# Block-causal attention and two expert layers on one core: head B's key blocks in reversed order

## The chip, the core and the metric

The kernel runs on one core of a Trainium2 chip. The metric is the time of one execution on the device in microseconds, median of three runs. The engines, named as in the profile, are PE (matmuls; PEld is its weight load), DVE and ACT (vector and scalar engine; both read and write PSUM, the matmuls' output memory of eight banks), POOL (elementwise work in SBUF) and SP (it only issues DMAs here).

## What is computed

Four batches of eight heads, 576 positions, 64 values a head. A query block of 64 sees the key blocks up to its own. The result goes through two expert layers.

```
scores = scale * q @ k.T          # per batch and head, 576 x 576
scores = where(block_i >= block_j, scores, -1e9)      # blocks of 64
attn = softmax(scores); x = (attn @ v), heads side by side: 2304 x 512
h = x @ w_in;  solu = h * softmax(h);  x = layernorm(solu) * g_ln @ w_out      # d_ff 1024
h = x @ w2_in; out = (h * tanh(softplus(h))) @ w2_out                          # d_ff 2048
```

## The kernel before, in words

**A planner sets the order.** The program adds operations with an engine, a cost, what they read and write, and a priority; `Plan.order` runs them through a list of events and emits every engine's instructions in the order that comes out. Priorities come from the table `PRIO` (lines 27 to 41) as base + step x index. On the chip each engine keeps its written order and waits by semaphores.

**Attention** (`pair`, line 533) works on two heads x = 0, 1 (A and B) of a batch at a time, 16 pairs. Loads (lines 539 to 558) bring q, k and v as 128 rows x 5 tiles x 2 heads x 64. `turn` (566) transposes k and q on PE, both heads at once; ACT and DVE split them into a high and a low part. The queries are shifted by 64, so that query tile t (0 to 4) sees EXT[t] = 64, 192, 320, 448 or 576 keys, and its first 64 rows don't see the last 64 of these. Scores (`mm`, 586) take three matmuls each, head A on the upper 64 rows of the array and head B on the lower. DVE masks and takes the maximum (617 to 641), ACT takes the exponential (603), DVE sums and inverts (597, 599), POOL normalises (649).

**Packs.** The normalised probabilities of tile t and head x lie in a tile of EXT[t] + 64 columns, the last 64 zero (memset once, 513). PE transposes them in pieces of 128 x 128 (688), in the four packs of line 521, for each head apart: 4 + 4 + 4 + 3 pieces. ACT (698) or DVE (695) copies each pack from PSUM to `ptw`. The products with v (`pv`, 658 to 677) come in two groups, queries 0 to 319 behind the second pack and 320 to 575 behind the fourth; each product has 128 keys, and the two heads lie on 64 columns of the array each. All of this is in f32; the scores and the layers use fp32r.

**The layers.** Tiles of 128 positions go through the first layer (`moe1_tile`, lines 744 to 798; `moe1_x2`, 806) as soon as a batch's attention is done. Its weights, and those of the second layer, are 64-bit floats that ACT, DVE and POOL take apart and put together (`weight`, 377 to 452; 304, 310). The second layer (901, 919) runs in two halves; its first half's weights lie where attention's buffers were, so they open when the last pair is done.

## Time and profile before

| | us |
|---|---|
| median of three runs (lowest, highest) | 836.85 (836.77, 838.5) |
| profiled execution | 836.64 |
| its span, first to last instruction | 834.9 |
| PE busy | 806.3 |
| ACT, DVE, POOL busy | 437.3, 435.8, 272.8 |

The span is 1.7 us shorter than the execution's own time. PE's busy time counts the stretch in which at least one matmul is in flight; matmuls overlap, so the mean length of one is longer than the step to the next. The mean granted clock of PE is 0.996.

### The profile page before, as it was taken

To read this page: it belongs to the slowest core of one execution; us is meant where nothing else is said; L and a number is where in the kernel's file an instruction comes from. 1 tells how busy PE (TensorE), PEld (TensorE's weight loads), DVE (VectorE), ACT (ScalarE), POOL (GpSimd) and SP (SyncE) were. 2 spreads that over 40 slices of the span, in tenths; PEclk is the share of its full clock that TensorE was granted. 3 is DMA by queue.
4 is the path that set the end of the run, shared out by engine and by line. 5 is a ranking of instruction groups with operands and counts; after the bars stand their busy time and mean duration, and the time that the engine had idled before them with its cause. 6 is when DMAs were issued, how large, how long until landed. Compare 5 with 4: busy or idle time off the path is not lost.

```text
span 834.9 us, 13619 instructions
## 1 busy us (share of the span) xinstructions
PE 806.3 (97%) x5184; PEld 708.3 (85%) x5184; DVE 435.8 (52%) x845; ACT 437.3 (52%) x944; POOL 272.8 (33%) x338
## 2 busy tenths in 40 slices
PE   4789999999999999999999999999999999999998
PEld 4667778887887898989898898999999989999996
DVE  7899999766755335899815687311111122112121
ACT  5889698656654334666636776532424323323230
POOL 4669888642533322331113432310202202102000
PEclk9899999999999999999999999999999999999999
DMA  8744334222200103433114635202202023031121
GB/s 202 166 112 120 109 95 110 47 60 71 50 26 15 40 14 112 154 126 114 64 57 133 214 102 177 75 1 76 74 3 75 21 94 114 2 114 41 35 76 38
DMA packets 88369, 69.54 MB, mean 83 GB/s; under 512 B 64496, under 2 KB 75248, under 8 KB 88304
## 3 DMA queue, kind: packets, MB, share of 16 engines
q1 hardware_dynamic: 88304, 68.67, 28.1%
q8 instruction: 41, 0.67, 0.3%
q14 instruction: 24, 0.20, 0.1%
HBM read 54.50 MB, written 14.16 MB: 82 GB/s over the span
## 4 chain that ended last, share of the span: by engine, by line
PE 76%; DVE 11%; ACT 6%; DMA 3%; issue 2%; POOL 1%; SPq 0%; ACTq 0%; DVEq 0%; POOLq 0%
PE ps L901 23%; PE ps L919 22%; PE ps L744 8%; PE ps L806 8%; PE ps L665 4%; PE ps L688 4%; PE ps L591 4%; ACT pt L603 2%; PE ps L567 1%; PE ps L790 1%; DMA wraw<-in_moe_w_in_dram 1%; DVE st L758 1%; DVE ptw L695 1%; DVE ps L433 1%; DVE e L765 1%
## 5 line engine op out<-in xcount | busy, mean ns | idle before, releaser
L310 DVE TENSOR_TENSOR gl<-s,gh 128x384 fp32r<-128x384 f32 x96 | 61.7, 646 | 254.9 <-ACT gh L304 254.8
L910 ACT ACTIVATE s<-ps 128x384 f32<-128x384 f32 x96 | 46.8, 490 | 199.1 <-PE ps L901 198.8
L313 POOL TENSOR_TENSOR x2l<-x2r,x2h 128x384 fp32r<-128x384 f32 x48 | 51.1, 1100 | 234.7 <-ACT x2h L304 227.6
L649 POOL TENSOR_SCALAR pt<-pt,sm 128x320 f32<-128x320 f32 (+4 forms) x160 | 89.8, 584 | 62.3 <-DVE sm L599 55.3
L603 ACT ACTIVATE pt<-ps,nmx 128x576 f32<-128x576 f32 (+4 forms) x160 | 82.9, 542 | 13.7 <-DVE nmx L618 6.0
L806 PE MATMUL ps<-lth,woh 128*128 128x256 f32 x288 | 81.6, 283 | 1.2 <-DVE ltl L310 1.2
L806 PE MATMUL ps<-lth,wol 128*128 128x256 f32 x288 | 80.0, 278 | 0.0
L806 PE MATMUL ps<-ltl,woh 128*128 128x256 f32 x288 | 79.9, 278 | 0.0
L901 PE MATMUL ps<-x2h,w2iha 128*128 128x384 f32 x192 | 64.7, 337 | 1.1 <-ACT s L910 0.8
L901 PE MATMUL ps<-x2h,w2ila 128*128 128x384 f32 x192 | 64.5, 336 | 0.0
L901 PE MATMUL ps<-x2h,w2ilb 128*128 128x384 f32 x192 | 64.4, 335 | 0.0
L901 PE MATMUL ps<-x2h,w2ihb 128*128 128x384 f32 x192 | 64.4, 335 | 0.0
L901 PE MATMUL ps<-x2l,w2iha 128*128 128x384 f32 x192 | 64.3, 335 | 0.0
L901 PE MATMUL ps<-x2l,w2ihb 128*128 128x384 f32 x192 | 64.3, 335 | 0.0
L688 PE MATMUL ps<-ident,pt 128*128 128x128 f32 x480 | 60.5, 277 | 1.1 <-ACT pt L603 0.8
L688 PEld LDWEIGHTS ps<-ident,pt 128*128 128x128 f32 x480 | 53.3, 142 | 6.3 <-issue 3.3
L806 PEld LDWEIGHTS ps<-lth,woh 128*128 128x128 f32 x288 | 54.1, 188 | 3.7 <-DVE ltl L310 2.1
L665 PE MATMUL ps<-ptw,vraw 128*64 128x256 f32 (+2 forms) x512 | 56.8, 365 | 0.3 <-DVE ptw L695 0.2
L919 PE MATMUL ps<-w2oha,gl 128*128 128x512 f32 x144 | 56.5, 393 | 0.0
L919 PE MATMUL ps<-w2ola,gh 128*128 128x512 f32 x144 | 56.5, 392 | 0.0
L919 PE MATMUL ps<-w2ohb,gl 128*128 128x512 f32 x144 | 56.4, 392 | 0.0
L919 PE MATMUL ps<-w2olb,gh 128*128 128x512 f32 x144 | 56.4, 392 | 0.0
(114 smaller groups left out, 1983.2 us busy)
## 6 DMA issues: line engine op xcount, KB each, us to landing
wraw<-in_moe_w_in_dram SPq DMA_DIRECT2D x24, 512.0 KB, 4.3
wraw<-in_moe_w_out_dram SPq DMA_DIRECT2D x24, 512.0 KB, 3.8
x2r<-x_d SPq DMA_DIRECT2D x12, 768.0 KB, 4.7
kraw<-in_k_dram SPq DMA_DIRECT2D x31, 160.0 KB, 3.1
qraw<-in_q_dram SPq DMA_DIRECT2D x31, 160.0 KB, 3.2
x_d<-xo SPq DMA_DIRECT2D x18, 256.0 KB, 2.2
acc_d<-ob SPq DMA_DIRECT2D x18, 256.0 KB, 2.2
ac<-acc_d SPq DMA_DIRECT2D x18, 256.0 KB, 3.9
```

Source lines behind the costliest of these rows:

```text
L310: nc.vector.tensor_tensor(out=dst, in0=src, in1=hi.bitcast(F32), op=ALU.subtract)
L313: nc.gpsimd.tensor_tensor(out=dst, in0=src, in1=hi.bitcast(F32), op=ALU.subtract)
L591: nc.tensor.matmul(out=dst, lhsT=a.t[hs, t * P:(t + 1) * P], rhs=m.t[hs, c0:c1], start=(i == 0), stop=(i == 2))
L603: add(ACT, c_act(EXT[t], acc=True), lambda: nc.scalar.activation(out=pp.t[:, 0:EXT[t]] if t < 4 else pp.t[:, 0:EXT[t]].rearrange("p (a c) ...
L649: nc.gpsimd.tensor_scalar(pp, pp, sm.t[:, x, t:t + 1], 1.0, op0=ALU.mult, op1=ALU.mult)
L665: nc.tensor.matmul(out=ps(s)[x * D:(x + 1) * D, o:o + n_], lhsT=vr.t[:, j, x, :], rhs=packs[pi].t[:, x, a:a + n_], start=(i == 0), stop=(i ...
L688: nc.tensor.transpose(ps2(s)[:, x, i * P:(i + 1) * P], pts[t][x].t[:, j * P:(j + 1) * P], ident)
L744: nc.tensor.matmul(out=ps2(hp)[:, hf, :], lhsT=x.t[:, kk, :], rhs=w[:, kk, hf * 512:(hf + 1) * 512], start=bool(first), stop=bool(last))
L806: nc.tensor.matmul(out=ps(s)[:, (c % 2) * 256:(c % 2) * 256 + 256], lhsT=w[:, kk, cs], rhs=x.t[:, kk, :], start=(kk == 0 and i == 0), stop ...
L901: nc.tensor.matmul(out=h(), lhsT=w[wk][:, kk, ms], rhs=x.t[:, kk, :], start=(kk == 0 and i == 0), stop=(kk == KD - 1 and i == 2))
L910: add(ACT, c_act(G2), lambda: nc.scalar.activation(out=s.t, in_=h(), func=AF.Mish), r=[hk, LEFT], w=[s.key()], rel=[hp], prio=pri("f_v" + ...
L919: nc.tensor.matmul(out=ps(oslots[t]), lhsT=x.t[:, tsl], rhs=w[wk][:, m, :], start=(m == 0 and i == 0), stop=(m == n - 1 and i == 2))
```

## The change

Head B's keys are loaded with their blocks of 64 in reversed order (`load_k`), its values with the halves of each 128 rows swapped to match. For query tile t head B then uses the last EXT[t] key columns, and the block that is masked for half the rows lies first. Both heads' probabilities of a tile share one buffer of 2 x EXT[t] columns, A's ahead of B's, so that A's last block and B's last block lie side by side, and one 128 x 128 transpose turns both. The zero columns go, with their memsets. There are three packs of 8, 8 and 9 transposes; two are copied by ACT, one by DVE. One operation holds all products: six per head over 128 keys (`OFFS`), then for each tile and head one over 64 keys, head A on the first 64 rows and columns of the array and head B on the last 64 of both. It waits for all three packs and takes two banks. Scores of tiles 2 and 1 change places in their bank pair, and POOL normalises in the order 4, 3, 2, 1, 0. The table of priorities is another one throughout.

```diff
 PRIO = {
-    "load_k": (3504.94, 0.69), "load_q": (3601.34, 2.86), "load_v": (10764.44, 18.27), "tr": (1871.2, 0),
...
+    "load_k": (2508.37, 65.35), "load_q": (2386.26, 352.01), "load_v": (3551.6, 0.07), "tr": (2558.2, 60.53),
+    "te": (2672.56, 73.32), "sc": (3442.57, 0.01), "mx": (363.67, 453.95), "ex": (3739.18, 0.11),
...
@@ -501,16 +501,12 @@
         nc.vector.memset(kraw.tiles[i][64:128, QT - 1], 0.0)
-        nc.vector.memset(vraw.tiles[i][64:128, QT - 1], 0.0)
...
-    NPT, NPTW = (4, 4, 4, 4, 3), 5
-    pt_r = [Rot(at, f"pt{t}_", NPT[t], (P, EXT[t] + 64), F32) for t in range(QT)]
-    for t in range(QT):
-        for i in range(NPT[t]):
-            nc.vector.memset(pt_r[t].tiles[i][:, EXT[t]:EXT[t] + 64], 0.0)
+    NPT, NPTW = (2, 2, 2, 2, 2), 5
+    pt_r = [Rot(at, f"pt{t}_", NPT[t], (P, 2 * EXT[t]), F32) for t in range(QT)]
@@ -518,17 +514,24 @@
-    PACKS = [
-        [(0, 0), (1, 0), (2, 0), (2, 2)],
-        [(1, 1), (2, 1), (3, 0), (4, 0)],
-        [(3, 1), (4, 1), (3, 2), (4, 2)],
-        [(3, 3), (4, 3), (4, 4)],
-    ]
-    RUNS = (
-        (320, 0, [(0, 0, 64, 320, 0), (1, 1, 0, 256, 64), (2, 0, 384, 128, 192)]),
-        (256, 320, [(0, 1, 256, 256, 0), (1, 2, 0, 256, 0), (2, 2, 256, 256, 0), (3, 3, 0, 256, 0),
-                    (4, 3, 256, 128, 128)]),
+    PACKS = (
+        [(t, 0, x, x, (t - 1) * P) for x in range(2) for t in range(1, QT)],
+        [(t, 1, x, x, (t - 2) * P) for x in range(2) for t in range(2, QT)] + [(4, 3, x, x, 384) for x in range(2)],
+        [(t, 2, x, 0, (t - 3) * P + 256 * x) for x in range(2) for t in range(3, QT)]
+        + [(t, t, 2, 1, 64 * t) for t in range(QT - 1, -1, -1)],
     )
+    PACKW = (1024, 1024, 512 + 384)
+
+    OFFS = (
+        (0, 0, 0, ((0, 0), (1, 0)), 256, 64), (0, 1, 1, ((0, 0), (1, 0)), 128, 192),
+        (1, 0, 0, ((0, 256), (1, 256)), 256, 0), (1, 1, 1, ((0, 128), (1, 128)), 256, 0),
+        (1, 2, 2, ((0, 0), (0, 256)), 256, 0), (1, 3, 1, ((0, 384), (1, 384)), 128, 128),
+    )
+    RUNS = ((0, 320), (320, 256))
@@ -552,10 +555,31 @@
-        for tag, r, src, off, pad in (("load_k", kr, k, 0, False), ("load_q", qr, q, -64, False), ("load_v", vr, v, 0, True)):
+        def load_k():
+            blocks = k[b, 2 * h2 + 1].rearrange("(j p) d -> p j d", p=64)
+            nc.sync.dma_start(out=kr.t[0:64, :, 1, :], in_=blocks[:, 8::-2, :])
+            nc.sync.dma_start(out=kr.t[64:128, 0:4, 1, :], in_=blocks[:, 7::-2, :])
+
+        m, go = load(lambda: kr.t[:, :, 0, :], k, n0 * S, False)
+        add(SP, 0.92, go, w=[kr.key(0)], prio=pri("load_k", p))
+        add(SP, 1.06, load_k, w=[kr.key(1)], prio=pri("load_k", p))
+        for x in range(2):
+            rows = v[b, 2 * h2 + x]
+
+            def go(x=x, rows=rows):
+                if x:
+                    blocks = rows.rearrange("(j p) d -> p j d", p=64)
+                    nc.sync.dma_start(out=vr.t[64:128, :, 1, :], in_=blocks[:, 0:9:2, :])
+                    nc.sync.dma_start(out=vr.t[0:64, 0:4, 1, :], in_=blocks[:, 1:9:2, :])
+                else:
+                    nc.sync.dma_start(out=vr.t[:, 0:4, 0, :], in_=rows[0:512, :].rearrange("(j p) d -> p j d", p=P))
+                    nc.sync.dma_start(out=vr.t[0:64, 4, 0, :], in_=rows[512:S, :])
+
+            add(SP, 1.06, go, w=[vr.key(x)], prio=pri("load_v", p))
-        pts = [[x.next(), x.next()] for x in pt_r]
+        pts = [x.next() for x in pt_r]
...
+                    o = (S - EXT[t]) * x
+                    nc.tensor.matmul(out=dst, lhsT=a.t[hs, t * P:(t + 1) * P], rhs=m.t[hs, o + c0:o + c1],
...
-            pp = pts[t][x]
+            pp = pts[t]
             add(ACT, c_act(EXT[t], acc=True), lambda: nc.scalar.activation(
-                out=pp.t[:, 0:EXT[t]] if t < 4 else pp.t[:, 0:EXT[t]].rearrange("p (a c) -> p a c", a=2), in_=src(),
+                out=pp.t[:, x * EXT[t]:(x + 1) * EXT[t]] if t < 4
+                else pp.t[:, x * EXT[t]:(x + 1) * EXT[t]].rearrange("p (a c) -> p a c", a=2), in_=src(),
...
-        for ts in (((3, 0), (0, 448)), ((2, 0), (1, 320))):
+        for ts in (((3, 0), (0, 448)), ((1, 0), (2, 192))):
@@ -632,10 +658,15 @@
-            add(DVE, 0.105 * len(ms), lambda s=s, ms=ms: [nc.vector.memset(
-                ps2(s)[0:64, :, o + EXT[t] - 64:o + EXT[t]], NEG) for t, o in ms], w=[sk], prio=pri("mx", p))
+            def mask(t, o, s):
+                a, d = o + EXT[t] - 64, S - EXT[t]
+                nc.vector.memset(flat(s, a + 2 * d)[0:64, a:].rearrange("p (x c) -> p x c", x=2)[:, :, 0:64], NEG)
+
+            add(DVE, 0.105 * len(ms), lambda s=s, ms=ms: [mask(t, o, s) for t, o in ms], w=[sk], prio=pri("mx", p))
-        for t in (4, 3, 0, 2, 1):
+        for t in (4, 3, 2, 1, 0):
-
-        def pv(ri, w, c0, items):
-            s = Slot()
-            ok, xk = ("o", p, ri), xt.key(h2, ri)
-
-            def go():
-                for i, (j, pi, a, n_, o) in enumerate(items):
-                    for x in range(2):
-                        nc.tensor.matmul(
-                            out=ps(s)[x * D:(x + 1) * D, o:o + n_], lhsT=vr.t[:, j, x, :],
-                            rhs=packs[pi].t[:, x, a:a + n_], start=(i == 0), stop=(i == len(items) - 1))
-
...
-        for pi, pk in enumerate(PACKS):
-            w = len(pk) * P
+        for pi, (pk, w) in enumerate(zip(PACKS, PACKW)):
             th = ptw_r.next()
             s = Slot(2)
             sk = ("pT", p, pi)
 
-            def tr(s=s, pk=pk):
-                for i, (t, j) in enumerate(pk):
-                    for x in range(2):
-                        nc.tensor.transpose(ps2(s)[:, x, i * P:(i + 1) * P], pts[t][x].t[:, j * P:(j + 1) * P], ident)
-
-            add(PE, 0.218 * len(pk) + 0.1 * (len(pk) < 4), tr, r=[pts[t][x].key() for t, _ in pk for x in range(2)], w=[sk, th.key()],
+            def turns(s=s, pk=pk):
+                for t, j, x, a, o in pk:
+                    c = t if x == 2 else 2 * t - j if x else j
+                    nc.tensor.transpose(ps2(s)[:, a, o:o + P], pts[t].t[:, c * P:(c + 1) * P], ident)
+
...
-            a = 64 if pi == 0 else 0
-            if pi % 2:
-                add(DVE, c_dve(2 * (w - a)), lambda s=s, a=a, w=w, th=th: nc.vector.tensor_copy(
-                    th.t[:, :, a:w], ps2(s)[:, :, a:w]), r=[sk], w=[th.key()], rel=[s], prio=pri("pe", p))
+            if pi == 1:
+                add(DVE, c_dve(w), lambda s=s, w=w, th=th: nc.vector.tensor_copy(
+                    th.t.rearrange("p a c -> p (a c)")[:, 0:w], flat(s, w)), r=[sk], w=[th.key()], rel=[s], prio=pri("pe", p))
             else:
-                add(ACT, c_act(2 * (w - a)), lambda s=s, a=a, w=w, th=th: nc.scalar.activation(
-                    out=th.t[:, :, a:w], in_=ps2(s)[:, :, a:w], func=AF.Copy), r=[sk], w=[th.key()], rel=[s], prio=pri("pe", p))
+                add(ACT, c_act(w), lambda s=s, w=w, th=th: nc.scalar.activation(
+                    out=th.t.rearrange("p a c -> p (a c)")[:, 0:w], in_=flat(s, w), func=AF.Copy), r=[sk], w=[th.key()],
+                    rel=[s], prio=pri("pe", p))
...
-            for ri in range(2):
-                if pi == max(it[1] for it in RUNS[ri][2]):
-                    pv(ri, *RUNS[ri])
+
+        os_ = [Slot(), Slot()]
+        oks = [("o", p, 0), ("o", p, 1)]
+        xks = [xt.key(h2, 0), xt.key(h2, 1)]
+
+        def pv():
+            for i, (r, j, pi, at_, n_, o) in enumerate(OFFS):
+                for x, (a, c0) in enumerate(at_):
+                    nc.tensor.matmul(
+                        out=ps(os_[r])[x * D:(x + 1) * D, o:o + n_], lhsT=vr.t[:, j, x, :],
+                        rhs=packs[pi].t[:, a, c0:c0 + n_], start=(i in (0, 2)), stop=False)
+            for t in range(QT):
+                c0, r = (P * t, 0) if t < 3 else (P * t - 320, 1)
+                for x in range(2):
+                    hs = slice(x * D, (x + 1) * D)
+                    nc.tensor.matmul(
+                        out=ps(os_[r])[hs, c0:c0 + 64], lhsT=vr.t[hs, t, x, :],
+                        rhs=packs[2].t[hs, 1, 64 + 64 * t:128 + 64 * t], start=False, stop=(t in (2, 4)))
+
+        add(PE, 4 * 1600 / 2370.0 + 0.25, pv, r=[vr.key(0), vr.key(1)] + [x.key() for x in packs], w=oks + xks, acq=os_,
+            prio=pri("pv", p))
...
```

What the order of the instructions shows, at three places. On SP, the first DMAs of the program before (kraw, qraw, vraw hold a pair's k, q, v; wraw a piece of weights):

```order
L399 DMA wraw_88<-in_moe_w_in_dram 128x512
L399 DMA wraw_89<-in_moe_w_in_dram 128x512
L542 DMA kraw_94<-in_k_dram 128x5x64 x2
L542 DMA kraw_95<-in_k_dram 128x5x64 x2
L547 DMA qraw_92<-in_q_dram 64x64
L551 DMA qraw_92<-in_q_dram 128x4x64
L542 DMA qraw_92<-in_q_dram 128x5x64
L399 DMA wraw_88<-in_moe_w_in_dram 128x512
```

and after the change:

```order
L550 DMA qraw_92<-in_q_dram 64x64
L554 DMA qraw_92<-in_q_dram 128x4x64
L545 DMA qraw_92<-in_q_dram 128x5x64
L545 DMA kraw_94<-in_k_dram 128x5x64
L560 DMA kraw_94<-in_k_dram 64x5x64
L561 DMA kraw_94<-in_k_dram 64x4x64
L545 DMA kraw_95<-in_k_dram 128x5x64
L560 DMA kraw_95<-in_k_dram 64x5x64
L561 DMA kraw_95<-in_k_dram 64x4x64
```

and on SP, following at once, down to the first weights:

```order
L545 DMA qraw_93<-in_q_dram 128x5x64 x2
L545 DMA kraw_94<-in_k_dram 128x5x64
L560 DMA kraw_94<-in_k_dram 64x5x64
L561 DMA kraw_94<-in_k_dram 64x4x64
L545 DMA kraw_95<-in_k_dram 128x5x64
L560 DMA kraw_95<-in_k_dram 64x5x64
L561 DMA kraw_95<-in_k_dram 64x4x64
L399 DMA wraw_88<-in_moe_w_in_dram 128x512
L399 DMA wraw_89<-in_moe_w_in_dram 128x512
```

The two pieces of weights that stood first now stand behind the q and k loads of two pairs and the k loads of two more; head B's k takes two DMAs of 64 rows in place of one of 128.

On PE, the transposes of the last columns of tiles 3 and 4 for the first pair (pt_0 is head A's tile, pt_1 head B's; 124 is tile 3, 128 tile 4), before:

```order
L688 MATMUL ps_66<-ident,pt_0_124 128x128
L688 MATMUL ps_66<-ident,pt_1_125 128x128
L688 MATMUL ps_66<-ident,pt_0_128 128x128
L688 MATMUL ps_66<-ident,pt_1_129 128x128
L688 MATMUL ps_66<-ident,pt_0_128 128x128
L688 MATMUL ps_66<-ident,pt_1_129 128x128
```

and the last pack after the change (110 to 118 are tiles 0 to 4, each with both heads):

```order
L696 MATMUL ps_64<-ident,pt_0_116 128x128
L696 MATMUL ps_64<-ident,pt_0_118 128x128
L696 MATMUL ps_64<-ident,pt_0_116 128x128
L696 MATMUL ps_64<-ident,pt_0_118 128x128 x2
L696 MATMUL ps_64<-ident,pt_0_116 128x128
L696 MATMUL ps_64<-ident,pt_0_114 128x128
L696 MATMUL ps_64<-ident,pt_0_112 128x128
L696 MATMUL ps_64<-ident,pt_0_110 128x128
```

Three pieces for each head became nine transposes: four that turn one head's columns and, last, one for each of the tiles 4 to 0 that turns both heads at once. The pieces of tiles 0, 1 and 2 that these replace stood in the other packs.

On PE, the products with v of the first pair (ptw is a pack), before:

```order
L665 MATMUL ps_64<-ptw_150,vraw_96 64x320 x2
L665 MATMUL ps_64<-ptw_151,vraw_96 64x256 x2
L665 MATMUL ps_64<-ptw_150,vraw_96 64x128 x2
L665 MATMUL ps_64<-ptw_151,vraw_96 64x256 x2
L665 MATMUL ps_64<-ptw_152,vraw_96 64x256 x4
L665 MATMUL ps_64<-ptw_153,vraw_96 64x256 x2
L665 MATMUL ps_64<-ptw_153,vraw_96 64x128 x2
```

and after the change:

```order
L717 MATMUL ps_64<-ptw_120,vraw_96 64x256 x2
L717 MATMUL ps_64<-ptw_121,vraw_96 64x128 x2
L717 MATMUL ps_64<-ptw_120,vraw_96 64x256 x2
L717 MATMUL ps_64<-ptw_121,vraw_96 64x256 x2
L717 MATMUL ps_64<-ptw_122,vraw_96 64x256 x2
L717 MATMUL ps_64<-ptw_121,vraw_96 64x128 x2
L724 MATMUL ps_64<-ptw_122,vraw_96 64x64 x10
```

Sixteen products of 128 to 320 columns became twelve of 128 or 256 and ten of 64. In the trace each of these f32 products is two records.

## Rows read from the trace of the kernel before

**Rows 1.** The page, part 1: busy us of each engine, share of the span, instructions

```profile
PE 806.3 (97%) x5184; PEld 708.3 (85%) x5184; DVE 435.8 (52%) x845; ACT 437.3 (52%) x944; POOL 272.8 (33%) x338
```

**Rows 2.** Busy us of each engine by stretch (length first), then PE clock, DMA share, GB/s

```profile
0.00:20.00 20.00, 10.04 (x60) 8.59 (x61) 14.85 (x52) 11.30 (x20) 7.83 (x12) 1.00 0.89 211
20.00:40.00 20.00, 14.88 (x117) 12.26 (x116) 16.60 (x37) 17.83 (x54) 13.33 (x21) 0.83 0.74 169
40.00:60.00 20.00, 17.39 (x164) 13.38 (x161) 18.81 (x36) 16.84 (x48) 12.48 (x16) 1.00 0.50 121
60.00:80.00 20.00, 19.02 (x181) 14.54 (x181) 18.93 (x41) 18.51 (x49) 17.39 (x25) 1.00 0.32 83
80.00:100.00 20.00, 19.37 (x129) 15.03 (x126) 18.30 (x35) 15.38 (x37) 17.03 (x19) 1.00 0.42 121
...
360.00:480.00 120.00, 115.97 (x731) 105.50 (x730) 79.20 (x148) 72.50 (x129) 33.05 (x32) 1.00 0.36 117
...
800.00:835.00 35.00, 31.17 (x158) 27.97 (x156) 6.52 (x11) 8.15 (x16) 0.00 (x0) 1.00 0.16 51
```

**Rows 3.** The page's costliest groups: count, busy us, mean ns of one, idle before, releaser

```profile
L688 PE MATMUL ps<-ident,pt 128*128 128x128 f32 x480 | 60.5, 277 | 1.1 <-ACT pt L603 0.8
...
L665 PE MATMUL ps<-ptw,vraw 128*64 128x256 f32 (+2 forms) x512 | 56.8, 365 | 0.3 <-DVE ptw L695 0.2
```

**Rows 4.** The chain of waits, 125 to 215 us: start us, us, what

```profile
160.50 1.75 PE ps L688 x16
162.25 1.40 PE ps L744 x6
...
177.17 2.10 PE ps L665 x20
179.27 1.90 PE ps L688 x16
...
183.53 1.34 PE ps L665 x12
...
202.05 3.28 PE ps L665 x32
205.33 1.59 PE ps L744 x6
```

**Rows 5.** Timeline of PE, 149 to 153 us: start us, us, engine, line, operation, count

```profile
149.93 0.19 PE L591 MATMUL ps<-kh,qh 64*128 64x64 f32 x2
149.96 0.27 PE L591 MATMUL ps<-kh,ql 64*128 64x64 f32 x2
150.06 0.28 PE L591 MATMUL ps<-kl,qh 64*128 64x64 f32 x2
```

**Rows 6.** Timeline of all engines, 0 to 14 us (SPq is the queue that issues DMAs)

```profile
0.72 0.86 SPq L399 DMA_DIRECT2D wraw<-in_moe_w_in_dram  x2
...
1.63 4.52 SPq L542 DMA_DIRECT2D kraw<-in_k_dram  x4
...
6.19 0.57 SPq L547 DMA_DIRECT2D qraw<-in_q_dram  x1
...
8.02 1.30 PE L567 MATMUL ps<-ident,kraw 128*128 128x128 f32 x5 [8.02 <-DMA kraw<-in_k_dram]
```

**Rows 7.** DMA issues: count, KB each, median us from issue to landing

```profile
qraw<-in_q_dram SPq DMA_DIRECT2D x31, 160.0 KB, 3.2
```

**Rows 8.** Timeline of PE, 0 to 60 us: the first products with v

```profile
39.05 3.35 PE L665 MATMUL ps<-ptw,vraw 128*64 128x320 f32 x32
```

**Rows 9.** The chain of waits, 355 to 475 us

```profile
367.70 4.79 DMA wraw<-in_moe_w_in_dram
```

**Rows 10.** Groups by shape: evictions of the packs and memsets of the start

```profile
L695 DVE COPY ptw<-ps 128x768 f32<-128x768 f32 x16 | 15.2, 951 | 5.4 <-PE ps L688 3.8 <-ACT pt L603 1.4
L698 ACT ACTIVATE ptw<-ps 128x896 f32<-128x896 f32 x16 | 15.0, 938 | 6.2 <-PE ps L688 6.2
...
L513 DVE MEMSET pt<- 128x64 f32 x19 | 1.4, 112 | 0.1
```

More of the change, by code (lines that the diff above doesn't have):

```diff
@@ L553, in load @@
             return 2, go
-        for tag, r, src, off, pad in (("load_k", kr, k, 0, False), ("load_q", qr, q, -64, False), ("load_v", vr, v, 0, True)):
+        def load_k():
[5 more added lines that the diff above has]
+        add(SP, 1.06, load_k, w=[kr.key(1)], prio=pri("load_k", p))
+        for tag, r, src, off, pad in (("load_q", qr, q, -64, False),):
             for x in range(2):
@@ L590, in mm @@
                     hs = slice(x * D, (x + 1) * D)
-                    nc.tensor.matmul(out=dst, lhsT=a.t[hs, t * P:(t + 1) * P], rhs=m.t[hs, c0:c1],
+                    o = (S - EXT[t]) * x
+                    nc.tensor.matmul(out=dst, lhsT=a.t[hs, t * P:(t + 1) * P], rhs=m.t[hs, o + c0:o + c1],
                                      start=(i == 0), stop=(i == 2))
@@ L647, in norm @@
         def norm(x, t):
[L648 removed]
+            pp = pts[t].t[:, x * EXT[t]:(x + 1) * EXT[t]]
             nc.gpsimd.tensor_scalar(pp, pp, sm.t[:, x, t:t + 1], 1.0, op0=ALU.mult, op1=ALU.mult)
[L651 removed]
+        for t in (4, 3, 2, 1, 0):
             for x in range(2):
[L653 removed]
+                add(POOL, c_ts(EXT[t]) + 0.08, lambda x=x, t=t: norm(x, t), r=[sm.key(x, t)], w=[pts[t].key(x)],
                     prio=pri("nm", p))
         packs = []
[L658 to L680 removed]
+        for pi, (pk, w) in enumerate(zip(PACKS, PACKW)):
             th = ptw_r.next()
@@ new lines, in pair @@
+        add(PE, 4 * 1600 / 2370.0 + 0.25, pv, r=[vr.key(0), vr.key(1)] + [x.key() for x in packs], w=oks + xks, acq=os_,
+            prio=pri("pv", p))
+        for r, (c0, w) in enumerate(RUNS):
+            if r:
+                add(DVE, c_dve(w), lambda c0=c0, w=w: nc.vector.tensor_copy(xt.t[:, h2, c0:c0 + w], ps(os_[1])[:, 0:w]),
+                    r=[oks[1]], w=[xks[1]], rel=[os_[1]], prio=pri("po", p))
+            else:
+                add(ACT, c_act(w), lambda c0=c0, w=w: nc.scalar.activation(
+                    out=xt.t[:, h2, c0:c0 + w], in_=ps(os_[0])[:, 0:w], func=AF.Copy), r=[oks[0]], w=[xks[0]],
+                    rel=[os_[0]], prio=pri("po", p))
```

37 lines of the change are left out of this document (14 added, 23 removed), and 7 rows, old and new, of the table PRIO.

## Prediction

> **What bounds the kernel now.** I read the page's busy times first, then the busy times by stretch, then the chain of waits and the timelines. [rows 1]: PE (the matmul engine) is busy 97% of the span, DVE and ACT 52%. So a microsecond of PE work taken out of a stretch in which PE never waits is a microsecond of time, and the question is where it waits. [rows 2] tell: in the first 100 us PE is idle for 9.96 + 5.12 + 2.61 + 0.98 + 0.63 = 19.3 us, between 360 and 480 us for 4.0, at the end for 3.8, and almost nowhere else. In the first 100 us the others are full instead: DVE 18.8, 18.9 and 18.3 of 20 us between 40 and 100, ACT 17.8 and 18.5 in two of the stretches. The start is therefore limited by latency and by DVE and ACT, the rest by PE.
>
> **Transposes of the probabilities.** Before, a pair takes 15 tiles for each head, 30 in all; now 8 + 8 + 9 = 25. In a full run sixteen take 1.75 us, 0.109 each [rows 4]; the group's mean of 277 ns [rows 3] is one instruction's length, overlapped with the next. 80 x 0.109 = **8.7 us** of PE work go. The nine of the last pack read both heads' halves of one tile and so wait for both norms, but they stood last before too.
>
> **Products with v.** In the trace each of these f32 matmuls is two records, so the 512 of [rows 3] are 16 products a pair. They stand in two groups, x12 with 704 columns a head and x20 with 1152, which take 1.34 and 2.10 us [rows 4]; the difference gives 0.76 / 448 = 1.70 ns a column (both heads run side by side on 64 columns of the array each) and 0.15 us for a group. Who comes next pays too: six L744 take 1.59 behind a product group and 1.40 elsewhere, sixteen L688 1.90 and 1.75 [rows 4]; I take 0.17. Thirteen pairs pay 1.34 + 2.10 + 2 x 0.17 = 3.78 us, three have one group of x32 at 3.28 + 0.17 = 3.45: 59.5 us together.
>
> Now a pair has one group: 1280 columns a head on all 128 rows, 1280 x 1.70 + 0.15 = 2.32 us, then ten products of 64 columns on a quarter of the array, whose price the trace doesn't have. Bounds: if the quarters of the two heads run side by side, 320 x 1.70 = 0.54 us; if one after the other, 1.09. The nearest rows are the 64-column scores, two heads on the two halves of the rows: 0.03 us from the first such couple to the second and 0.10 to the third [rows 5]. The columns themselves need no more than 0.03, so something else (the load of 128 columns of weights, I think) sets the longer step. A quarter has 64 columns of weights, half of that, 0.05 us a couple and 0.54 for ten couples. Both ways of reading the row lie within the bounds; I take 0.54, because every couple of heads in the trace that uses separate parts of the array runs side by side. A change from half array to quarter array gets 0.17 like the others. 2.32 + 0.17 + 0.54 + 0.17 = 3.20, sixteen times 51.2: **8.3 us** less. With quarters in turn it is 8.6 more, a loss of 0.3.
>
> One rule speaks against 0.54. The row shows only couples that write two different banks [rows 5]; here two row halves of the array write one bank, on different partitions. The Trainium skill, TensorEngine Tiling (Array Packing), section Restrictions and Gotchas, says that different row tiles cannot access the same PSUM bank simultaneously. By that the quarters would go in turn, and the sum would be 8.6 us worse. The Trainium skill's page PSUM — Partial Sum Buffer, section Terms, lets different groups of 32 partitions of a bank be accessed at the same time; by that the sum stands. No row here shows either.
>
> **The start.** The order of the queue changes: q and k of two pairs go first and the first weights behind them. The first matmul starts at 8.02 us, held by k's load, which was issued behind two weight loads and took 4.52 us to issue four [rows 6]. Alone, an issue is 0.57 us [rows 6] and q lands 3.2 us later [rows 7]: three issues from 0.7 us on and the landing give 0.7 + 1.7 + 3.2 = 5.6 for the last, or some 5.1 if it counts from the last issue's start; 2.9 us earlier. The weights' preparation on ACT, DVE and POOL then stands behind two pairs' work, and DVE loses a copy of 768 columns a pair, 0.951 us [rows 10]: 4.8 us for the five pairs or so of the first 100 us, on the engine that is full there. The first products with v start at 39.05 us [rows 8]. Of the 11.3 us that PE waits after its first matmul I take 5 back: **8 us** in all. Bounds: nothing (ACT's work for a pair is the same, and ACT is nearly as full), and 12.2, all of the 9.3 us after 20 us and the 2.9.
>
> **The late stall.** The 4.0 us that PE is idle from 360 to 480 us I put down to the second layer's weights: the chain runs through their load for 4.79 us there [rows 9], and their buffers open when the last pair is done. In the order before, 648 of the first layer's 1296 matmuls stand behind the last pair's products, now 936, so the loads have longer cover. I take half, **2 us** (bounds 0 and 4).
>
> **Edits at nothing.** The memsets at the start, 1.4 us for nineteen of the 21 [rows 10], run while DVE waits for the first weights; without that cover they cost as much. The mask is one memset for both heads as before, at another column. The sixteen more k loads cost 0.57 us each on SP, which has nothing else to do than issue; if q or v came late for it in every pair, that is 9 us at most. The products now wait for all three packs of a pair; behind them on PE stand the next pair's scores, and whoever needs the freed banks. The order puts other matmuls between the last pack and the products, and ACT's copy of it out of PSUM (0.94 us for 896 columns, [rows 10]) fits under two score groups. Half as many probability tiles mean that the scores two pairs on wait for the transposes; the order has those far ahead.
>
> **Sum.** The profiled execution took 836.64 us (span 834.9); the median of the runs is 0.2 above it, so no correction. 836.6 - 8.7 - 8.3 - 8 - 2 = **809.6 us**.
>
> **Rivals.**
> - *Quarters in turn.* For: the page's rule, and the 0.10 us step of [rows 5], which a quarter may keep. Against: all other couples run side by side. 809.6 + 8.6 = 818.2 us. Chance 0.17.
> - *The start gives nothing.* ACT takes DVE's place: 17.8, 16.8 and 18.5 of 20 us busy from 20 to 80 us [rows 2], and every pair still asks the same of it. PE then works less and waits more there. 817.6 us. Chance 0.2. Both together: 826.2, chance 0.06.
> - *Slower: each small product waits for the one before to leave the array.* Two row halves that add into one bank in turn might drain each time. The place is the ten products' twenty records, the price the full length of a 64-column record, 0.27 us [rows 5]: 5.4 in place of 0.54, 4.9 x 16 = 78 more, 888 us. It decides from 27.0 / 16 = 1.69 us a pair on, that is from (0.54 + 1.69) / 20 = 0.11 us a record. Against it: records of couples overlap everywhere in the trace. Chance 0.05.
> - *No net change.* The reordering stalls PE in the middle for as much as it saves, about 27 us where [rows 2] now show almost none; or the quarter mode is not what runs. Chance 0.03.
>
> **How the numbers follow.** The forecast has 0.49. All terms at their best: 12.2 for the start, 4 for the late stall, no charge for the inner mode change (2.7): 836.6 - 8.7 - 11.0 - 12.2 - 4 = 801. All bad bounds together: 836.6 - 8.7 + 0.3 = 828. From 801 to 828 lie the forecast and the first three cases, 0.92. A measurement here tells about 0.2% (1.7 us) from no change. Faster by more: 0.92; within: 0.03; slower: 0.05.
>
> **What would show it.** 400 transposes in place of 480, at 0.109 us. A product group of 24 records and 20 small ones: about 2.9 us from the first to the next group if side by side, about 3.4 if in turn, over 4.6 if the slow rival is right; the small ones' starts in couples a few ns apart with 0.05 us between couples. The first matmul at 5 us, the first products with v near 32 us. Idle PE time of about 11 us in the first 100 us, under 3 between 360 and 480. I am wrong if PE shows new idle time between 100 and 360 us, or if the small products take over 0.1 us a couple.

## The result, and the profile after

The changed kernel takes **823.7 us** (median of 4 runs, 823.15 to 825.36) beside 836.85 for the kernel before on the same chip: a ratio of 0.9842, interval 0.9823 to 0.986. That is faster by 13.15 us, where 27.2 were forecast. The time lies inside the range (801 to 828), but the forecast was missed by 14 us. The profiled execution has a span of 821.4 us, 13.5 less than before. An execution more than 1.5% slower than the fastest of its kernel is left out of the times below (one, of e4).

The page of the changed kernel, part 1 (as [rows 1]):

```profile
PE 790.0 (96%) x5296; PEld 699.2 (85%) x5296; DVE 418.1 (51%) x808; ACT 435.6 (53%) x944; POOL 272.3 (33%) x338
```

The text calls PE TensorE, DVE VectorE, ACT ScalarE and POOL GpSimd. TensorE's work fell by 16.3 us (806.3 to 790.0; 17.0 were forecast for transposes and products). So the shortfall is not in the work. It is in the waiting: span less busy time was 28.6 us and is 31.4, where the forecast had it fall by 10.

Busy times by stretch of the kernel before (columns as in [rows 2]):

```profile
0.00:80.00 80.00, 61.32 (x511) 48.77 (x513) 69.19 (x163) 64.49 (x167) 51.03 (x73) 0.96 0.61 146
80.00:180.00 100.00, 98.38 (x769) 78.90 (x766) 85.31 (x174) 77.32 (x184) 73.74 (x92) 1.00 0.36 93
180.00:260.00 80.00, 79.52 (x669) 68.15 (x668) 47.73 (x99) 47.64 (x129) 29.70 (x54) 1.00 0.17 42
260.00:360.00 100.00, 99.95 (x740) 87.71 (x739) 59.96 (x116) 47.92 (x84) 34.81 (x44) 1.00 0.25 78
```

The same stretches of the changed kernel, and the one that answers to the sixth of [rows 2]:

```profile
0.00:80.00 80.00, 66.51 (x665) 54.90 (x665) 67.09 (x150) 66.18 (x178) 51.33 (x77) 0.98 0.65 149
80.00:180.00 100.00, 90.36 (x814) 72.51 (x815) 89.11 (x180) 83.04 (x213) 71.98 (x99) 0.98 0.39 101
180.00:260.00 80.00, 80.00 (x724) 70.63 (x722) 45.55 (x98) 47.98 (x112) 40.20 (x58) 1.00 0.12 34
260.00:360.00 100.00, 96.40 (x668) 85.62 (x666) 82.62 (x153) 59.11 (x97) 30.69 (x34) 1.00 0.37 119
360.00:480.00 120.00, 119.14 (x730) 108.85 (x729) 57.13 (x101) 61.88 (x113) 32.97 (x31) 1.00 0.29 92
```

Read the first busy column against the length. TensorE's idle time went from 18.7 to 13.5 us in the first 80, from 1.6 to **9.6** between 80 and 180, from 0.1 to 3.6 between 260 and 360, and from 4.0 to 0.9 between 360 and 480. The gain at the start is taken back in the next 100 us. VectorE is busy 89 of 100 us there (85 before), and 83 of 100 between 260 and 360, where it was 60.

Whom TensorE waits for between 80 and 180 us (us in total, times, longest; the kernel before has 1.3 us in three waits there):

```profile
PE ps L696 <- DVE kl L310: 4.6, 4, 3.1
PE ps L591 <- ACT pt L628: 1.7, 3, 0.7
PE ps L778 <- ACT pt L628: 0.8, 1, 0.8
PE ps L616 <- ACT pt L628: 0.7, 1, 0.7
```

The waits behind kl, on VectorE, are 4.6 us; those behind pt, ScalarE's exponentials, are 3.5 with one more of 0.3. The longest is worth following. The chain of waits of the changed kernel, 77 to 96 us (start us, us, what):

```profile
77.00 1.29 DVE nmx L670 x2
...
80.26 0.94 ACT pt L628 x3
81.23 1.09 DVE sm L622
82.98 1.29 DVE nmx L670 x2
84.27 1.67 DVE wil L310
85.95 1.41 DVE wem L401
87.35 0.68 DVE kl L310
88.07 1.20 PE ps L696 x9
89.28 2.44 PE ps L778 x6
```

For 11 us the chain does not touch TensorE at all. The transposes of the last pack (L696 x9) need two banks of PSUM. The instruction that makes kl (L310) gives two back, and it stands on VectorE behind two instructions on weights (wil and L401's wem) that have nothing to do with this pair. The timelines of VectorE and of GpSimd in those microseconds show why these two are so long:

```profile
81.23 1.08 DVE L622 TENSOR_SCALAR sm<-sm 128x2 f32<-128x2 f32 x1 [0.32 <-ACT pt L628]
...
84.19 1.76 DVE L310 TENSOR_TENSOR wil<-wem,wih 128x512 fp32r<-128x512 f32 x1
85.87 1.48 DVE L401 TENSOR_SCALAR wem<-wraw 128x512 int32<-128x512 int32 x1
87.27 0.75 DVE L310 TENSOR_TENSOR kl<-ps,kh 128x576 fp32r<-128x576 f32 x1
```

```profile
81.00 1.27 POOL L450 TENSOR_TENSOR wem<-wem 128x512 f32<-128x512 f32 x1
...
84.11 1.28 POOL L448 TENSOR_TENSOR wem<-wem,wraw 128x512 f32<-128x512 f32 x1
85.47 1.59 POOL L450 TENSOR_TENSOR wem<-wem 128x512 f32<-128x512 f32 x1
```

L622 works on 2 columns and usually takes 0.17 us. Here it takes 1.08, and its end, 82.31, is that of GpSimd's L450 (82.27). wil usually takes 0.64 to 0.78 us and 1.76 here, L401 0.42 and 1.48. In the whole trace several VectorE instructions that read only SBUF, the memory in which the tiles lie (L310 on wil and gl, L401, L403, L445, L464, L622), are at times stretched like this, and only where GpSimd was at work when they began. Those that read PSUM never are, though GpSimd was running at the start of 13 of the 16 instructions on ql. The Trainium skill, SBUF — State Buffer, section Who interferes with whom, says that a VectorE instruction with two SBUF inputs contends with a GpSimd instruction that reads SBUF; the same section of the Trainium skill describes an exclusive lock for the length of an instruction. The rows agree for wil and L445 beside GpSimd's L448. They don't beside GpSimd's L680, which reads SBUF too: there L445 took its usual 0.66 to 0.68 us three times (at 36.07, 57.60 and 68.09 us). For L401 and L622, with one input, the other condition that this section of the Trainium skill names (a two-port mode) would have to hold, which no row shows.

TensorE stands for 3.07 us, and after it the granted clock is 0.73 between 90 and 95 us, that is half rate (1.2 in place of 2.4 GHz) for about half of that stretch. In e6 below, TensorE is busy throughout 85 to 95 us, and the granted clock there is 1.00.

### The profile page after: what moved, and what is told of

Its sections match the earlier page's. It is cut to its first block, busy times and chain, and to the rows that moved or that the text cites. A ratio compares the mean times of both kernels' runs of the same rounds, so it can differ in the third digit from the quotient of the medians.

```text
span 821.4 us, 13863 instructions
## 1 busy us (share of the span) xinstructions
PE 790.0 (96%) x5296; PEld 699.2 (85%) x5296; DVE 418.1 (51%) x808; ACT 435.6 (53%) x944; POOL 272.3 (33%) x338
## 4 chain that ended last, share of the span: by engine, by line
PE 72%; DVE 16%; ACT 7%; DMA 3%; issue 2%; SPq 1%; DVEq 0%; ACTq 0%
PE ps L935 24%; PE ps L953 23%; PE ps L840 8%; PE ps L778 6%; ACT pt L628 4%; PE ps L696 3%; PE ps L616 3%; PE ps L717 3%; DVE nmx L670 2%; DMA wraw<-in_moe_w_out_dram 2%; DVE st L792 1%; DVE wem L403 1%; PE ps L824 1%; DVE ps L433 1%; DVE wem L401 1%
## 5 line engine op out<-in xcount | busy, mean ns | idle before, releaser
L310 DVE TENSOR_TENSOR gl<-s,gh 128x384 fp32r<-128x384 f32 x96 | 57.0, 599 | 269.9 <-ACT gh L304 269.7
L680 POOL TENSOR_SCALAR pt<-pt,sm 128x448 f32<-128x448 f32 (+4 forms) x160 | 90.6, 586 | 64.0 <-DVE sm L624 20.3
L628 ACT ACTIVATE pt<-ps,nmx 128x320 f32<-128x320 f32 (+4 forms) x160 | 83.2, 548 | 18.3 <-DVE nmx L670 9.5
L696 PE MATMUL ps<-ident,pt 128*128 128x128 f32 x400 | 51.4, 279 | 8.1 <-DVE kl L310 6.0
L696 PEld LDWEIGHTS ps<-ident,pt 128*128 128x128 f32 x400 | 44.6, 143 | 13.8 <-DVE kl L310 6.8
L953 PE MATMUL ps<-w2oha,gh 128*128 128x512 f32 x144 | 56.1, 390 | 0.1
L953 PE MATMUL ps<-w2ohb,gh 128*128 128x512 f32 x144 | 56.0, 389 | 0.0
```

Source lines behind the costliest of these rows:

```text
L310: nc.vector.tensor_tensor(out=dst, in0=src, in1=hi.bitcast(F32), op=ALU.subtract)
L628: add(ACT, c_act(EXT[t], acc=True), lambda: nc.scalar.activation(out=pp.t[:, x * EXT[t]:(x + 1) * EXT[t]] if t < 4 else pp.t[:, x * EXT[t] ...
L680: nc.gpsimd.tensor_scalar(pp, pp, sm.t[:, x, t:t + 1], 1.0, op0=ALU.mult, op1=ALU.mult)
L696: nc.tensor.transpose(ps2(s)[:, a, o:o + P], pts[t].t[:, c * P:(c + 1) * P], ident)
L953: nc.tensor.matmul(out=ps(oslots[t]), lhsT=x.t[:, tsl], rhs=w[wk][:, m, :], start=(m == 0 and i == 0), stop=(m == n - 1 and i == 2))
```

## The experiments

The question was where the new 9.6 us come from: the change's order of work, its buffers and banks, or an engine that is late in any case. Idle times are TensorE's, length of the stretch less its busy time; 0 to 180 us sums to 20.3 us for the kernel before and 23.1 for the changed one. Times are compared by their ratio to the kernel before on the same chip. Runs e3, e4, e5, e6, e9, e10 and e11 keep the order of the changed kernel's instructions on every engine; what is cut, repeated or added is named.

### e1 and e2: the two tables swapped

e1 is the changed kernel with the table `PRIO` of the kernel before, e2 the reverse. The first line of e1's table:

```diff
-    "load_k": (2508.37, 65.35), "load_q": (2386.26, 352.01), "load_v": (3551.6, 0.07),
+    "load_k": (3504.94, 0.69), "load_q": (3601.34, 2.86), "load_v": (10764.44, 18.27),
```

> The changed kernel with the table of priorities of the kernel before: the change's instructions in an order that spreads the 16 pairs as before. Two theories on the idle time that TensorE shows after the change between 80 and 180 us (9.6 us of 100, 1.6 before). THEORY ORDER: it comes from the new order, which packs the pairs denser (last pair's VectorE copy at 264 us, 324 before), so that VectorE frees the banks too late. Then the old order on the new structure loses TensorE little in that stretch (idle 4 us or less in 80 to 180 us), and the time is 812 to 820 us. THEORY STRUCTURE: it comes from what the change does to buffers and banks (two probability buffers in place of four, one product group that needs all three packs and two banks at once), which stalls TensorE in any order. Then the idle time of 80 to 180 us stays at 8 us or more, and the time is 823 us or above.

> The kernel before with the change's table of priorities, nothing else. THEORY ORDER: the denser order brings TensorE's waits into the old structure too: idle of 6 us or more between 80 and 180 us (1.6 in the kernel before), and a time of 840 to 850 us, in spite of a start that may come sooner. THEORY STRUCTURE: the idle time of 80 to 180 us stays under 3 us, and the time is 828 to 837 us, the earlier start kept.

e1: 840.92 us, 1.0054 (1.0025 to 1.0083). e2: 854.77 us, 1.0218 (1.0198 to 1.0238). The stretch of 80 to 180 us in e1, then in e2:

```profile
80.00:180.00 100.00, 91.86 (x853) 74.58 (x852) 83.68 (x176) 81.23 (x209) 77.37 (x106) 0.97 0.36 90
```

```profile
80.00:180.00 100.00, 90.95 (x668) 71.26 (x665) 83.37 (x173) 77.71 (x180) 77.05 (x93) 0.97 0.35 91
```

e1 came out as "structure" said (8.1 us of idle time, above 823 us), e2 as "order" said in its idle time (9.1 us), with a time above its 850. So each theory is contradicted by one of the two. What follows is less than either said: a table fits the structure for which it was made, and on the other structure it costs some 18 us by the ratios (e1 against the changed kernel, e2 against the one before). That both swaps make TensorE wait says nothing yet on what it waits for. In e1 the largest waits of the stretch, 6.0 of the 8.1 us, are again behind kl; 4.1 of them are the products' (L717), which need two banks at once since the change.

### e3: less work on VectorE

```diff
-  out=nmx.t[:, x, 4:5], in_=ps2(s4[x])[:, :, 0:288], axis=AX.XY, op=ALU.max, negate=True),
+  out=nmx.t[:, x, 4:5], in_=ps2(s4[x])[:, :, 64:128], axis=AX.XY, op=ALU.max, negate=True),
-  out=nmx.t[:, :, t], in_=ps2(s)[:, :, o:o + EXT[t]], ...
+  out=nmx.t[:, :, t], in_=ps2(s)[:, :, o + 64 * (t > 0):o + 64 + 64 * (t > 0)], ...
```

> The changed kernel with every instruction in its place, but VectorE's maximum over a row of scores goes over 64 unmasked columns of it and not over all (softmax allows any number in that place). Some 2 us of VectorE's work per pair go, 30 us in all. THEORY ORDER, with VectorE as the limit: the idle time of TensorE between 80 and 180 us falls from 9.6 us to under 5, and the time to 814 to 819 us. THEORY STRUCTURE (buffers and banks, whoever frees them): the idle time stays within 2 us of 9.6, and the time is 821 to 825 us.

818.12 us, 0.9782 (0.9766 to 0.9798): 5.0 us faster, by the ratios, than the changed kernel, with TensorE's instructions untouched.

```profile
80.00:180.00 100.00, 94.06 (x880) 75.87 (x879) 81.32 (x189) 87.31 (x219) 79.56 (x106) 1.00 0.42 108
```

Idle there 5.9 us (under 5 was expected), from 0 to 180 us 18.4 in place of 23.1. VectorE is a limit of that stretch. This version also beats both kernels; it relies on no score being so far above the 64 looked at that the exponential overflows, which these inputs grant and others need not.

### e4: less work on VectorE, and no faster

```diff
-  add(DVE, 0.07, lambda: nc.vector.tensor_scalar(
-      sm.t[:, :, a:a + n_], sm.t[:, :, a:a + n_], 1e-9, None, op0=ALU.add), w=c, prio=pri("su", p))
+  add(DVE, 0.07, lambda: None,
+      w=c, prio=pri("su", p))
```

> The changed kernel in the same order without VectorE's 32 small additions of 1e-9 to the row sums of the scores (128x2x1 and 128x2x4 values), of which some lasted 1.1 us beside work of GpSimd and 0.17 elsewhere. THEORY ORDER, with VectorE as the limit and these small instructions, late behind GpSimd, as a part of it: 32 x 0.17 = 5.4 us of VectorE's work go, and 1 to 2 us more where they stretched; TensorE's idle time between 80 and 180 us falls by 2 to 4 us, and the time is 819.5 to 822 us. If the stretched instructions only fill time in which VectorE would wait anyway: within 1 us of the changed kernel's 823.7.

827.73 us (823.05 to 829.99), 0.9878 (0.9853 to 0.9903): neither time expected. It is some 3 us slower, by the ratios, than the changed kernel, little more than the noise. The idle time of 80 to 180 us falls by 2.4 us, as the first expectation said, but that of the first 80 rises by 4.0. VectorE, GpSimd and TensorE in this run:

```profile
71.81 5.40 DVE L401 TENSOR_SCALAR wem<-wraw 128x512 int32<-128x512 int32 x1
...
78.66 0.74 DVE L310 TENSOR_TENSOR kl<-ps,kh 128x576 fp32r<-128x576 f32 x1
```

```profile
70.55 1.29 POOL L448 TENSOR_TENSOR wem<-wem,wraw 128x512 f32<-128x512 f32 x1
71.83 1.46 POOL L680 TENSOR_SCALAR pt<-pt,sm 128x576 f32<-128x576 f32 x2
73.27 1.21 POOL L307 TENSOR_SCALAR xh<-xt 128x512 fp32r<-128x512 f32 x2
74.44 2.48 POOL L313 TENSOR_TENSOR xl<-xt,xh 128x512 fp32r<-128x512 f32 x2
```

```profile
79.46 1.76 PE L696 MATMUL ps<-ident,pt 128*128 128x128 f32 x7 [4.86 <-DVE kl L310]
```

The same L401 in the changed kernel:

```profile
71.01 0.41 DVE L401 TENSOR_SCALAR wem<-wraw 128x512 int32<-128x512 int32 x1
```

There it began beside GpSimd's L680, which started at 70.82, and took its usual time. Without the small instruction it begins while GpSimd is still in L448, 0.03 us before the end of that, and stands for 5.40 us, until 77.21, through seven GpSimd instructions without a gap, L448 the first (the last ends at 76.92). kl and then TensorE wait behind it: 4.86 us, and a granted clock of 0.50 between 80 and 85 us. In the profiled execution TensorE is idle 2.3 us longer than in the changed kernel (33.7, 31.4) and busy 4.5 us longer (794.5, 790.0), at a mean granted clock of 0.988 for 0.995. This one wait is longer than the 4.0 us that the idle time of the first 80 grows by, and it outweighs 5 us of VectorE's work less. So the timing of VectorE against GpSimd counts, and not VectorE's sum alone.

### e5: give TensorE its transposes back

```diff
-  for t, j, x, a, o in pk:
+  for t, j, x, a, o in pk + [y for y in pk if y[2] == 2]:
```

> The changed kernel in its order, but the five transposes per pair that the change saves are given back as repeats: the five of the shared diagonal blocks are issued twice, the second time over the first. TensorE gets 80 x 0.109 = 8.7 us of work, 60 of the 80 (6.5 us) before 180 us, where 12 of the 16 pairs are done. THEORY A, between 20 and 180 us TensorE waits for others and its saved work has turned into waiting: most of the 6.5 us falls into the 9.6 us of idle time there (idle of 80 to 180 us falls to 6 us or less), only the 2.2 us after 180 us cost in full, and the time rises by 1 to 5 us over the changed kernel's 823.7: 825 to 829 us. THEORY B, TensorE's work is what sets the time there too and the waits are by the side: the idle time stays within 1.5 us of 9.6 and the time rises by 7 to 9 us, to 831 to 833 us.

831.07 us, 0.9923 (0.9905 to 0.9942), 6.8 us above the changed kernel; between the two theories.

```profile
80.00:180.00 100.00, 92.91 (x843) 75.17 (x843) 86.77 (x179) 81.40 (x204) 71.12 (x101) 0.98 0.40 102
```

Against the changed kernel's profile TensorE is busy 11.2 us longer (801.2): 8.7 of repeats, by the price in the expectation, which leaves 2.5 for the lower mean granted clock (0.992 for 0.995). Idle time falls by 3.6 (31.4 to 27.8), 2.6 of it here. So, by this estimate, about 40% of the repeats fell into waits; the rest cost time. The test does not separate the theories as cleanly as it was meant to, since the clock took a part.

### e6: GpSimd out of VectorE's way

```diff
-  ... nc.gpsimd.tensor_tensor(out=mf(), in0=mf(), in1=lo().bitcast(F32), op=ALU.add), ...
+  ... nc.gpsimd.tensor_tensor(out=mf()[:, 0:16], in0=mf()[:, 0:16], in1=lo().bitcast(F32)[:, 0:16], op=ALU.add), ...
-  out=mf(), in0=mf(), in1=ex().bitcast(F32), op=ALU.mult), ...
+  out=mf()[:, 0:16], in0=mf()[:, 0:16], in1=ex().bitcast(F32)[:, 0:16], op=ALU.mult), ...
```

> The changed kernel in its order; the two GpSimd instructions that finish each chunk of the first layer's weights (an addition and a multiplication over 512 columns, 16 chunks up to 180 us, 1.3 us each) go over 16 columns alone. It leaves out most of that part of the weights. It takes some 38 us of GpSimd's work away and no work from VectorE. THEORY A, VectorE's instructions on SBUF alone stand still until GpSimd's instruction ends (the row sum 75.39 to 76.54 us ends with GpSimd's 76.51), and that is a part of why VectorE frees banks late: VectorE's excess over its usual durations in 0 to 180 us falls from 15.4 us to 9 or less, TensorE's idle time of 80 to 180 us from 9.6 to 7 us or less, and the time to 816 to 821 us. THEORY B, the stretched instructions only take up time in which VectorE would wait anyway: the excess falls too, but the idle time stays within 1.5 us of 9.6 and the time is 822 to 826 us.

816.38 us, 0.9747 (0.9731 to 0.9763): 8 us faster, by the ratios, than the changed kernel.

```profile
80.00:180.00 100.00, 94.81 (x887) 76.72 (x886) 84.57 (x190) 88.18 (x220) 56.88 (x105) 1.00 0.43 109
```

VectorE's excess over its usual durations (each instruction against the shorter quarter of its own kind, counted where it is over 0.2 us) falls from some 15 us to under 3 in the first 180, TensorE's idle time from 80 to 180 us from 9.6 to 5.2. The waits behind kl in that stretch, 4.6 us in the changed kernel, in e3 and then in e6:

```profile
PE ps L696 <- DVE kl L310: 3.1, 4, 1.4
```

```profile
PE ps L696 <- DVE kl L310: 0.9, 3, 0.3
```

Theory A holds: VectorE is late by its own work (e3) and by standing behind GpSimd (e6). The cut also makes each weight chunk ready sooner by some 2 us; TensorE's waits on weights were no part of the 9.6 us, but how much of the 8 us that adds was not tried.

### e7 and e8: other tables, for both kernels

The first line of e7's table, cut short (e8 is the kernel before with a table of the same make):

```diff
-    "load_k": (2508.37, 65.35), "load_q": (2386.26, 352.01), "load_v": (3551.6, 0.07), ...
+    "load_k": (8630.84, 13.7), "load_q": (-534.5, 2671.42), "load_v": (9437.42, 0.07), ...
```

> The changed kernel with another table of priorities, nothing else: it was searched for with VectorE's standing behind GpSimd priced in as the traces show it (an instruction on SBUF alone waits for the end of a two-operand one of GpSimd). THEORY A, the idle time of 80 to 180 us belongs to the change's table, which places VectorE's and GpSimd's work so that they collide: with another table the same structure shows 6 us of idle or less there (9.6 with the change's own), and takes 814 to 820 us. THEORY B, the waits come from the lighter TensorE work beside an unchanged amount of VectorE's and ScalarE's, whatever the table: the idle time stays at 8 us or more, or comes back in another stretch, and the time is 822 us or above.

> The control for the run before: the kernel before with a table of priorities from the same search. If the change's own table was simply less well fitted than that of the kernel before (THEORY A), the search finds little here: 833 to 838 us, and the change is worth more than 13 us between tables of equal care. If the search gains as much here as on the changed kernel (829 to 833 us), the change's own table was as good as the table before it, and the change is worth the 13 us that were measured.

e7: 822.88 us, 0.9817 (0.979 to 0.9844). e8: 833.86 us, 0.9962 (0.9946 to 0.9978). The first two stretches of e7:

```profile
0.00:80.00 80.00, 61.64 (x588) 53.63 (x588) 66.94 (x152) 68.52 (x181) 52.04 (x75) 1.00 0.68 156
80.00:180.00 100.00, 95.78 (x851) 79.50 (x849) 86.93 (x180) 83.70 (x201) 76.59 (x101) 0.98 0.39 93
```

Between 80 and 180 us the idle time falls to 4.2 as theory A said, but in the first 80 it rises to 18.4: 22.6 us together, as the 23.1 of the change's own table. The time is no different from the changed kernel's within the intervals. By its words theory B has it: the waiting comes back in another stretch. But the first DMA issues of e7 show another reason, a start with two loads of weights ahead of q:

```profile
0.72 0.87 SPq L399 DMA_DIRECT2D wraw<-in_moe_w_in_dram  x2
1.63 0.56 SPq L550 DMA_DIRECT2D qraw<-in_q_dram  x1
```

The first matmul comes at 8.06 us and the first products at 38.12 (4.84 and 31.55 in the changed kernel, 8.02 and 39.05 in the one before). So e7 gives up the early start, and that waits only move, whatever the table, is not shown: a table with the early start and the 4.2 us was not tried.

e8 starts as early as the changed kernel (4.90 and 31.70 us) and has 14.9 us of idle time in the first 80, 3.8 less than the kernel before. So most of what the change gained there comes from its table and could be had without it. e8's time fell into the first range, but what was to follow from it (worth more than 13 us) did not come: between these two tables the change is worth 0.9962 to 0.9817, some 12 us, close to the 13 measured.

### e9, e10, e11: which engine, and what is behind it

e9 is e3 and e6 together, e11 has all three cuts, and e10 is this one alone (GpSimd sets the packs to zero at the start, five memsets, since most of them is no longer written):

```diff
-  out=th.t.rearrange("p a c -> p (a c)")[:, 0:w], in_=flat(s, w), func=AF.Copy)
+  out=th.t.rearrange("p a c -> p (a c)")[:, 0:64], in_=flat(s, 64), func=AF.Copy)
```

> The changed kernel in its order with both earlier cuts at once: VectorE's maximum over 64 columns (e3) and GpSimd's two weight instructions over 16 columns (e6; it leaves out most of that part of the weights). Alone they gave 5.6 and 7.3 us of 823.7. THEORY A, VectorE is late for two reasons of its own, its work and its standing behind GpSimd, and both are on the path: the gains nearly add up, 809 to 813 us, and TensorE's idle time from 0 to 180 us falls from 23.1 us to under 15. THEORY B, both shorten the same few waits, behind which something else (ScalarE, the start's loads) is next: 814 to 817 us, idle time of 0 to 180 us 16 to 18 us as in each alone (18.4 and 17.5).

> The changed kernel in its order, with ScalarE's two copies of packs per pair (1024 and 896 columns, 0.93 and 1.03 us) over 64 columns alone; it leaves out most of the probabilities that the products with v read. Some 1.6 us a pair, 26 us in all, of ScalarE's work go, VectorE's stays. The rival of the prediction was that ScalarE takes VectorE's place. If ScalarE is a limit of the first 180 us beside VectorE, or the copy stands on the chain from transposes to products: idle time of 0 to 180 us from 23.1 to 19 us or less, time 814 to 820 us. If VectorE alone is late there: idle time within 2 us of 23.1 and 822 to 825 us.

> The changed kernel in its order with the cuts of e3, e6 and e10 together: some 34 us less on VectorE, 26 on ScalarE, 38 on GpSimd, TensorE's work as it was. If these engines set the waits of the first 180 us: idle time there 12 us or less, which is little more than the start up to the first products, and 804 to 809 us, about what was forecast. If the loads and the chain of one pair set them: idle time 15 us or more and 811 us or above.

The stretch of 80 to 180 us in e9, e10 and e11:

```profile
80.00:180.00 100.00, 96.06 (x902) 78.05 (x900) 71.59 (x191) 89.38 (x221) 59.58 (x107) 1.00 0.43 110
```

```profile
80.00:180.00 100.00, 90.99 (x851) 73.74 (x847) 90.99 (x184) 76.85 (x219) 75.40 (x101) 1.00 0.40 102
```

```profile
80.00:180.00 100.00, 97.14 (x911) 78.97 (x910) 73.10 (x196) 80.60 (x220) 59.25 (x108) 1.00 0.43 109
```

| run | us | ratio to before, interval | idle 0 to 80 | 80 to 180 | 0 to 180 | mean granted clock |
|---|---|---|---|---|---|---|
| before | 836.85 | | 18.7 | 1.6 | 20.3 | 0.996 |
| changed | 823.7 | 0.9842 (0.9823 to 0.986) | 13.5 | 9.6 | 23.1 | 0.995 |
| e3, VectorE | 818.12 | 0.9782 (0.9766 to 0.9798) | 12.5 | 5.9 | 18.4 | 0.996 |
| e6, GpSimd | 816.38 | 0.9747 (0.9731 to 0.9763) | 12.3 | 5.2 | 17.5 | 0.996 |
| e9, both | 814.45 | 0.9737 (0.9695 to 0.9779) | 12.3 | 3.9 | 16.3 | 0.998 |
| e10, ScalarE | 821.93 | 0.9818 (0.9785 to 0.9851) | 14.9 | 9.0 | 24.0 | 0.996 |
| e11, all | 814.09 | 0.9724 (0.9681 to 0.9766) | 10.3 | 2.9 | 13.2 | 0.992 |

ScalarE's copies alone move nothing: 20.6 us less of its work (435.6 to 415.0; 26 were expected) leave the idle time at 24.0 and the time within the intervals of the changed kernel. The five memsets add 4.5 us of work to GpSimd's first 20 us, which may hide a little. And this speaks for the copies only. The exponentials, behind which TensorE waits for 3.5 us between 80 and 180, were shortened in no run. VectorE's and GpSimd's cuts shorten mostly the same waits (theory B of e9: 16.3 us, not additive). Only with both out of the way does ScalarE's cut show: 16.3 to 13.2 us of idle time in e11. Its median does not follow, since TensorE is busy 2.1 us longer than in e9 (790.8, 788.7) at a lower mean granted clock (0.992 for 0.998); the one execution of e11 with a clock of 0.998 took 810.85 us, the two of e9 814.33 and 814.57. What remains is 7.4 us of the first 20 and 5.8 after them. That idle time lies between the two expectations of e11, the time in the second; no run took the rest apart.

## Why the prediction was wrong

- **Transposes (-8.7) and products (-8.3): right.** The page counts 400 transposes. The first products of the changed kernel (L717, the small ones L724), timeline of TensorE (as [rows 8]):

```profile
31.55 2.38 PE L717 MATMUL ps<-ptw,vraw 128*64 128x256 f32 x24
33.86 0.80 PE L724 MATMUL ps<-ptw,vraw 64*64 64x64 f32 x20
34.59 0.36 PE L616 MATMUL ps<-kh,qh 64*128 64x192 f32 x2
```

  The group takes 3.04 us to the next one (2.9 forecast), as do twelve of the sixteen, the quarters 0.73 with the change of mode: behind the first, couples start 0.058 us apart, the two heads 6 to 7 ns. They run side by side; 0.05 had been read out of [rows 5]. The rivals "quarters in turn" and "slower" fall with it. The rule that one bank cannot take two row tiles at once (the Trainium skill, TensorEngine Tiling (Array Packing), section Restrictions and Gotchas) does not show here: the heads write one bank on different partitions. The rule of the Trainium skill, PSUM — Partial Sum Buffer, section Terms, is the one with which the trace agrees.
- **The start (-8): right in kind, too large.** The first matmul comes at 4.84 us (5.1 forecast), the first products at 31.55 (32). The idle time of the first 80 us falls by 5.2, and that of the first 100, for which the prediction counted its 8 us, only by 2.0 (19.3 to 17.3): the long wait at 85 us lies there. VectorE was busy some 4 us less there, as the term expected (87.5 to 83.3 us), but it came late at 85 us all the same.
- **"The rest by PE": this step failed.** The prediction took TensorE for the bound after 100 us because it found little idle time there, and so counted each microsecond of its work there in full. Between 100 and 360 us the idle time was 1.5 us and is 9.4. Between 80 and 180 us VectorE was busy 85 of 100 in the kernel before already; TensorE's 98 hid that it had a second engine close behind. The change takes work from VectorE too (435.8 to 418.1 us in all), but its order does more pairs early: 295 of 400 transposes begin before 180 us, 277 of 480 in the kernel before, that is 11.8 pairs for 9.2. VectorE has the reductions, splits and copies of each, now in a stretch with GpSimd's work on the first layer's weights, and so is busy longer there (89.1 for 85.3 us). It comes late, and TensorE waits 8.0 us more between 80 and 180 us. e3 and e6 show the two parts of it (5.9 and 5.2 us of idle time in place of 9.6; 3.9 with both). No run gave TensorE another bank, so what the change's larger need of banks (the products take two at once) adds to a late VectorE is not shown.
- **The late stall (-2): moved, not removed.** From 360 to 480 us 3.2 us of idle time go, more than forecast, but 3.6 come between 260 and 360: more of the second layer's weights are now prepared there (L436 on VectorE 16 times, 6 before; VectorE 83 us of 100, 60 before), and TensorE waits for the first layer's work on VectorE (L778 for e of L799 1.8 us, L824 for ltl 1.1). No run took this apart. Net +0.4 in place of -2.
- **Sum.** -16.3 work, -5.2 start, +8.0, +3.6 - 3.2, and -0.5 between 180 and 260: -13.6, beside -13.5 in the span. With the prediction's border at 100 us it is -16.3 work (-17.0 forecast), -2.0 start (-8), +7.9 between 100 and 360 us (0) and -3.2 behind (-2). The rival "the start gives nothing" (817.6) had the kind of the loss, less work and more waiting, but named ScalarE taking VectorE's place, where e3 and e6 show VectorE itself, and let the loss stop at 8 us. The sign that was named for being wrong, new idle time between 100 and 360 us, is what came (and from 80 on). The rival "no net change" (chance 0.03) named the kind of place, stalls in the middle, but only at the size of the whole saving. That the time lies in the range is luck: the range was wide for the quarters and for the bounds of the start and the late stall, and not for waits between 100 and 360 us.

## What to carry to other kernels

Work taken from the busiest engine is worth its time only as long as the second engine of that stretch lets it be: before counting such a saving in full, read the busy times of the others in the same stretch, and count how many units of work the new order puts there. Where VectorE and GpSimd both work on SBUF, their busy shares do not add up independently: look for small VectorE instructions that last as long as GpSimd's neighbour, and see who stands behind them. And compare an order with an order that was fitted as well: a table made for another structure cost some 18 us here, more than the change is worth.
